# An attention and two MLPs on one core: 1/sqrt from a table, weight halves spread over the blocks, results kept in SBUF

## The chip, the core and the metric

The kernel runs on one NeuronCore of a Trainium2 chip. Its engines work from queues of their own, each in the order in which the program gives its instructions: PE (TensorE, matrix products), DVE (VectorE) and ACT (ScalarE) for elementwise work, POOL (GpSimd) and SP, which here issue transfers (DMAs). The metric is device time in microseconds (us) of one execution.

## The reference

```python
def _attn_ref(q, k, v, g_norm):          # q, k, v: (8, 8, 576, 64) fp32
    kv = np.einsum('bhsd,bhse->bhde', k, v)
    out = np.einsum('bhsd,bhde->bhse', q, kv)
    rms = np.sqrt(np.mean(out * out, axis=-1, keepdims=True) + 1e-06)
    return (out / rms * g_norm).astype(np.float32)
...
x = attn_out.transpose(0, 2, 1, 3).reshape(4608, 512)
gate = 1.0 / (1.0 + np.exp(-(x @ w_gate)))           # w_gate, w_val: 512 x 1536
x = (gate * (x @ w_val)) @ w_out                     # w_out: 1536 x 512
...
h = x @ w_in                                         # w_in: 512 x 2048
g = np.where(h >= 1, h, np.where(h <= -1, 0.0, (h + 1) ** 2 / 4))
return g @ w_out                                     # w_out: 2048 x 512
```

## The kernel before, in words

Every fp32 product is made as three products of fp32r halves: a value is split into a high half (`hi`, a copy on ACT) and the rest (`lo`, a subtraction on DVE), and `mm3` (L82 to L86) adds hi x hi, hi x lo and lo x hi. `split` (L70) is that pair of instructions.

The 4608 tokens are 9 blocks of 512. The first MLP takes a block in 12 chunks of 128 of its 1536 hidden columns. For a chunk, `gate_value` sums the gate into PSUM bank h0 and the value into bank h1 (12 matmuls each), ACT takes the sigmoid of h0 (L441), DVE multiplies it by h1 (L443, `gf`). `split_g` and `split_wo` make the halves gh, gl of that product and woh, wol of the output weights, and `down` adds the chunk's projection into four banks (12 matmuls). There is one h0 and one h1, so the next chunk's gate waits until the sigmoid has read the last.

The order in each queue is the order of the code. In blocks 2 to 7, chunk f issues in turn: the gate of chunk f + 1 with its sigmoid and splits; a piece of the next block's attention (`late_piece`; even chunks take one of four pairs of heads, odd chunks its norm: a sum of squares on PE, `inv_rms`, and later a Newton step); the projection of chunk f; and some steps of preparing the second MLP's weights (`w2_steps`). At a block's end, `store` evacuates the four banks and sends them to DRAM (`x2d`), and the next block's first gate follows.

The weights of the second MLP arrive as 64-bit floats. `decode_steps` turns a tile into fp32 on ACT and DVE in 6 steps. An "in" unit decodes two tiles, makes four sums and differences (for a Strassen-like product), and splits and stores four pairs of halves to `w2d`; an "out" unit decodes one, splits and stores it to `wo2d` (`halves_out`). There are 8 in and 16 out units. In `halves_out` each high half is written over a tile that the pair before has just stored, so a split waits until those stores have landed. Before, `run(work, 6)` follows each chunk and the rest of a block's three or four units is run at its end; the last three units lie in block 8.

Block 8's 12 products are stored to DRAM (`gd`) and loaded again for its projection, beside which the second MLP starts: `Second.begin` loads the first x (`x_load`) and the first weights (`w_load`, tile `wst`), and `x_steps` makes the x halves. The second MLP takes 6 groups of 768 tokens. A group has 8 chain sets of 7 products (`product`, L556) in banks A, B, C, D, each set with its own `wst` (1.8 MB, two buffers), and then 16 output products. A set's last product and the next set's first both use bank A.

Of the kernel before, what the change touches and what calls it, by code (L numbers as in the profile page):

```python
# [15 lines left out]
P = 128  # L16
# [16 lines left out]
def attn_gated_mlp_kernel(ctx: ExitStack, tc: tile.TileContext, a: dict, out: bass.AP):  # L33
# [45 lines left out]
    def temp(name, tag, **kw):  # L79
        return tp.tile([P, T], F32, name=name, tag=tag, **kw)  # L80
# [26 lines left out]
    def load_q(j, p, early=False):  # L107
        t = wp.tile([P, T], F32, name="q_early", tag="w") if early else temp("qraw", "qraw", bufs=2)
        nc.sync.dma_start(out=t, in_=a["qT"][p, :, j * T:(j + 1) * T])
        qraw[j, p] = t  # L110
# [52 lines left out]

    def inv_rms(SS, m, r):
        nc.vector.tensor_scalar(out=m, in0=SS, scalar1=1.0 / D, scalar2=EPS, op0=ALU.mult, op1=ALU.add)
        nc.scalar.activation(out=r, in_=m, func=AF.Sqrt)
        nc.vector.reciprocal(out=r, in_=r)

    def newton(m, r, t):

# [137 lines left out]
    def run(steps, n=None):  # L308

        while n != 0 and next(steps, steps) is not steps:  # L310
            n = n and n - 1
# [70 lines left out]
    def load_raw_w2():  # L382
        if w2_todo:
            key = w2_todo.pop(0)
            load_raw(key, a["w_2"][key[1:]])

    def halves_out(src, place, dst):

        hi, lo = place.bitcast(F32R), src.bitcast(F32R)
        yield split(src, hi, lo)  # L390
        for h, t in enumerate((place, src)):
            d = dst(h)
            nc.sync.dma_start(out=d, in_=t if len(d.shape) == 2 else t.rearrange("p (o n) -> p o n", n=2 * P))
        yield
        yield

    def w2_steps(unit):
# [30 lines left out]
    def gv_sum(f, i, xs, bank=None, between=None):  # L428
        if bank is None:
            t = h_p.tile([P, T], F32, name=f"h{i}", tag=f"h{i}")  # L430
        else:
            t = acc_p.tile([P, T], F32, name=f"h{i}", tag=f"acc{bank}")
        for c in range(KC):
            mm3(t, wgv[f, i], xs[c], c == 0, c == KC - 1, slice(c * P, (c + 1) * P))
            if between and c == KC // 2 - 1:
                run(between, 1)
        return t

    def gv_act(gate, value, tag="gf"):
        sig = temp("sig", "sig")  # L440
        nc.scalar.activation(out=sig, in_=gate, func=AF.Sigmoid)  # L441
        g = temp("gf", tag, bufs=1 if tag == "gf" else 2)
        nc.vector.tensor_tensor(out=g, in0=sig, in1=value, op=ALU.mult)  # L443
        return g

    def gate_value(f, xs, banks=(None, None), tag="gf"):
        return gv_act(*(gv_sum(f, i, xs, banks[i]) for i in range(2)), tag)

    def split_g(j, f, g):
        gs[j, f] = split(g, half_tile(gp, "gh", "gh"), half_tile(gp, "gl", "gl"))  # L450
# [16 lines left out]
    def store(dst, tags=("dt", "du", "dt", "du")):  # L467
        for c in range(4):
            t = temp("ev", tags[c], bufs=2 if tags[c] in ("dt", "du") else 1)
            (act_copy if c % 2 else dve_copy)(t, acc[c])  # L470
            nc.sync.dma_start(out=dst(c), in_=t)


    class Second:
# [23 lines left out]

        def bank(self, tag):
            return self.ch_p.tile([P, T], F32, name=f"ch{tag}", tag=tag)  # L500


        def w_load(self, s):
# [94 lines left out]
        def rest(self):  # L598
            self.wo2p = self.pool("wo2", 1, "left")
            self.gst = self.pool("gst", 1, "left")  # L600
            self.gsp = self.pool("gsp", 4, "left")
            self.acc_p = self.pool("acc2", 1, "left", space=bass.MemoryType.PSUM)
            self.wo2 = {}
            self.wo2_load(0)
            self.wo2_load(HF)
            groups = NT // (2 * T2)
            for g in range(groups):
                self.group(g, g + 1 < groups)
            self.stack.close()

        def group(self, g, more):
# [1 line left out]
            acc = [self.acc_p.tile([P, T], F32, name=f"acc2_{t}", tag=f"acc2_{t}") for t in range(3)]  # L613
            late = None
            for s in range(HF):
                A, D, B, C = (self.bank(n) for n in "ADBC")
                self.ws = self.w_next
                if s + 1 < HF:
                    self.w_next = self.w_load(s + 1)
                    if g == 0:  # L620
                        self.wo2_load(s + 1)
                        self.wo2_load(s + 1 + HF)
                elif more:
                    x = self.x_load(g + 1)
                c0 = self.tmp.tile([P, 2, T2], F32, name="c0", tag="c0", bufs=2)
# [51 lines left out]
            self.out_product(acc, HF - 1, this_hi, False, False)  # L677
            ready[1] = self.high(src(order[1]))
            self.low(ready[1], src(order[1]))
            acc2 = [self.bank("B"), self.bank("C"), self.acc_p.tile([P, T], F32, name="acc2_3", tag="acc2_3")]  # L680
            if more:
                steps = self.x_steps(x)
                self.w_next = self.w_load(0)
# [22 lines left out]
    with tc.manual_schedule():  # L706
# [197 lines left out]
            if f == F1 - 1:  # L904
                store(lambda c: x2d[j][:, c, :], ("du", "sig", "du", "gf"))
        split_wo(wo, 0)
        share = {j: n for j, n in zip(range(2, NB), (3, 4, 3, 4, 3, 4, 3))}

        def w2_work(j):
            for unit in w2_units[sum(share[i] for i in range(2, j)):][:share[j]]:  # L910
                yield from w2_steps(unit)

        last = NB - 1
        load_raw_w2()
        for j in range(2, last):
            work = w2_work(j)
            for f in range(F1):
                if j + 2 < B and f in (0, 2, 4, 6):
                    load_kv(j + 2, f // 2)
                if f + 1 < F1:  # L920
                    g = gate_value(f + 1, xs)
                    split_g(j, f + 1, g)
                    split_wo(wo, f + 1)
                if f < 9:
                    late_piece(j + 1, f)
                    if f % 2 and j + 2 < B:
                        kv_product(j + 2, f // 2)
                down(j, f)
                if f == F1 - 2:
                    split_x()  # L930
                run(work, 6)
                if f == F1 - 1:
                    run(work)
                    store(lambda c: x2d[j][:, c, :])
                    if j + 1 < last:
                        split_wo(wo, 0)
                        split_g(j + 1, 0, gate_value(0, xs))
                    if j + 2 < NB:
                        load_q(j + 2, 0)
                        load_q(j + 2, 1)  # L940

        work = w2_work(last)
        for f in range(F1):
            keep_g(0, f, gate_value(f, xs, tag="wol"))
            run(work, 6)
            if f >= F1 - 3:
                load_g(0, f - F1 + 3)
        run(work)
        early_end.close()
        second = Second()  # L950
        split_g(last, 0, gf[0, 0])
        split_wo(wo, 0)
        load_g(0, 3)
        second.begin()
        for f in range(F1):
            if f + 1 < F1:
                split_g(last, f + 1, gf[0, f + 1])
                split_wo(wo, f + 1)
            if 0 < f < F1 - 3:
                load_g(0, f + 3)  # L960
            if f > 1:
                run(second.xsteps, 1)
            down(last, f)
        store(lambda c: x2d[last][:, c, :])
        run(second.xsteps)
        first_part.close()
        second.rest()

# [39 lines left out]
```

## Time and profile before

| | |
|---|---|
| time, three runs | 1835.89 us median (1834.65 to 1841.38) |
| the profiled execution | 1834.16 us, span 1832.4 us |
| PE busy | 1771.7 us (97%) |
| DVE, ACT busy | 1092.5 us (60%), 790.8 us (43%) |
| mean granted clock of PE | 0.988 |
| DMA | 233.28 MB, all but 1.4 MB on SP's queue |

The span is the time from the first to the last instruction. "Idle before <- X" is the time that an engine stood before an instruction, and what released it. The granted clock is 1.00 at 2.4 GHz and 0.50 at 1.2 GHz. Blocks 0 and 1 run to about 300 us, blocks 2 to 7 from there to about 955, block 8 to 1062, the second MLP from there to the end.

### The profile page before, as it was taken

What the parts mean: (1) busy time and instruction counts of PE and PEld (TensorE: products, weight loads), DVE (VectorE), ACT (ScalarE), POOL (GpSimd) and SP (SyncE); (2) the same over time, 40 slices, a digit from 0 to 9 for tenths busy, and PEclk for the clock granted to TensorE, in tenths of its full rate; (3) what the DMA queues carried; (4) which work ended last, traced back from release to release, by engine and by line L of the source; (5) the groups of instructions that cost most, each with busy time, mean ns of one, the idle gap of its engine ahead of it and who ended that gap; (6) DMA issues with size and microseconds to landing.
All of it is one profiled execution on the core that took longest, in us unless ns stands there. A gap on an engine that the chain in (4) does not pass through costs nothing.

```text
span 1832.4 us, 22307 instructions
## 1 busy us (share of the span) xinstructions
PE 1771.7 (97%) x8560; PEld 1489.7 (81%) x8560; DVE 1092.5 (60%) x1817; ACT 790.8 (43%) x1361; POOL 2.0 (0%) x10
## 2 busy tenths in 40 slices
PE   8999999999989999999999899999999999999999
PEld 5787787787767887878778689889899898898897
DVE  3788756756657586665664545655555556456453
ACT  4454344534445455454542334434444344344342
POOL 0000000000000000000000000000000000000000
PEclk9999999999989999999999999999999999999999
DMA  7454633222242222211223466254344343342430
GB/s 220 151 194 161 208 101 112 86 89 85 74 130 89 77 90 92 77 63 58 86 71 136 161 248 250 82 188 153 113 165 163 103 159 130 138 161 93 178 121 35
DMA packets 85403, 233.28 MB, mean 127 GB/s; under 512 B 8488, under 2 KB 36264, under 8 KB 79152
## 3 DMA queue, kind: packets, MB, share of 16 engines
q1 hardware_dynamic: 85296, 231.85, 37.3%
q8 instruction: 67, 1.10, 0.2%
q14 instruction: 40, 0.33, 0.1%
HBM read 179.91 MB, written 51.90 MB: 127 GB/s over the span
## 4 chain that ended last, share of the span: by engine, by line
PE 50%; DVE 5%; DMA 3%; ACT 2%; issue 1%; SPq 0%; DVEq 0%; ACTq 0%
PE chA L556 8%; PE acc L86 6%; PE acc L85 6%; PE acc L84 6%; PE chB L556 5%; PE chD L556 3%; PE h L84 3%; PE chC L556 2%; PE h L86 2%; PE h L85 2%; DMA wst<-w2d 2%; PE chC L85 1%; PE chB L85 1%; PE chC L86 1%; PE chB L86 1%
## 5 line engine op out<-in xcount | busy, mean ns | idle before, releaser
L84 PE MATMUL h<-xh,w 128*128 128x512 f32 x768 | 307.3, 400 | 27.3 <-ACT sig L441 27.3
L86 PE MATMUL h<-xh,w 128*128 128x512 f32 x768 | 303.8, 396 | 0.2 <-DVE w L73 0.2
L85 PE MATMUL h<-xl,w 128*128 128x512 f32 x768 | 303.6, 395 | 0.0
L84 PEld LDWEIGHTS h<-xh,w 128*128 128x128 f32 x768 | 147.1, 192 | 66.6 <-ACT sig L441 35.1
L84 PE MATMUL acc<-gh,woh 128*128 128x512 f32 x432 | 178.0, 412 | 4.4 <-ACT woh L65 4.4
L86 PEld LDWEIGHTS h<-xh,w 128*128 128x128 f32 x768 | 147.0, 191 | 32.0 <-DVE w L73 0.6
L85 PE MATMUL acc<-gl,woh 128*128 128x512 f32 x432 | 171.7, 397 | 1.4 <-DVE gl L73 1.2
L86 PE MATMUL acc<-gh,wol 128*128 128x512 f32 x432 | 172.4, 399 | 0.5
L85 PEld LDWEIGHTS h<-xl,w 128*128 128x128 f32 x768 | 147.2, 192 | 30.6
L443 DVE TENSOR_TENSOR gf<-sig,h 128x512 f32<-128x512 f32 x108 | 74.0, 686 | 140.1 <-PE h L86 117.5
L86 PE MATMUL acc<-wo,gh 128*128 128x512 f32 x384 | 151.1, 393 | 0.0
L85 PE MATMUL acc<-wo,gh 128*128 128x512 f32 x384 | 150.9, 393 | 0.0
L84 PE MATMUL acc<-wo,gh 128*128 128x512 f32 x384 | 149.6, 389 | 0.0
L556 PE MATMUL chA<-x_t,wst 128*128 128x384 f32 x576 | 116.6, 337 | 0.0
L65 ACT ACTIVATE gh<-gf 128x512 fp32r<-128x512 f32 x72 | 45.6, 633 | 153.7 <-DVE gf L443 153.7
L441 ACT ACTIVATE sig<-h 128x512 f32<-128x512 f32 x108 | 64.1, 593 | 104.1 <-PE h L86 95.6
L556 PEld LDWEIGHTS chA<-x_t,wst 128*128 128x128 f32 x576 | 102.6, 188 | 3.7
L84 PEld LDWEIGHTS acc<-gh,woh 128*128 128x128 f32 x432 | 81.6, 189 | 25.0 <-ACT woh L65 5.3
L85 PEld LDWEIGHTS acc<-gl,woh 128*128 128x128 f32 x432 | 81.9, 190 | 22.1 <-DVE gl L73 2.8
L86 PEld LDWEIGHTS acc<-gh,wol 128*128 128x128 f32 x432 | 81.5, 189 | 22.0 <-DVE wol L73 2.8
L491 DVE TENSOR_TENSOR c<-chD,p 128x384 f32<-128x384 f32 x48 | 26.8, 558 | 110.6 <-ACT v L568 89.2
L65 ACT ACTIVATE u<-chA 128x384 f32<-128x384 f32 x96 | 47.1, 491 | 102.4 <-PE chA L556 102.4
(171 smaller groups left out, 3210.1 us busy)
## 6 DMA issues: line engine op xcount, KB each, us to landing
wst<-w2d SPq DMA_DIRECT2D x48, 1792.0 KB, 7.5
raw<-in_w SPq DMA_DIRECT2D x32, 512.0 KB, 4.6
raw<-in_w_gv SPq DMA_DIRECT2D x24, 512.0 KB, 4.4
kvraw<-in_kv_main SPq DMA_DIRECT2D x24, 448.0 KB, 4.6
gd<-gf SPq DMA_DIRECT2D x36, 256.0 KB, 3.4
gload<-gd SPq DMA_DIRECT2D x36, 256.0 KB, 3.0
x2d<-ev SPq DMA_DIRECT2D x36, 256.0 KB, 2.7
xin<-x2d SPq DMA_DIRECT2D x36, 256.0 KB, 4.9
```

The lines of the kernel that those rows point to most:

```text
L65: nc.scalar.activation(out=o, in_=i, func=AF.Copy)
L84: nc.tensor.matmul(ps, w[0][:, wsl], x[0], start=first, stop=False)
L85: nc.tensor.matmul(ps, w[0][:, wsl], x[1], start=False, stop=False)
L86: nc.tensor.matmul(ps, w[1][:, wsl], x[0], start=False, stop=last)
L441: nc.scalar.activation(out=sig, in_=gate, func=AF.Sigmoid)
L443: nc.vector.tensor_tensor(out=g, in0=sig, in1=value, op=ALU.mult)
L491: nc.vector.tensor_tensor(out=o, in0=x, in1=y, op=op)
L556: nc.tensor.matmul(bank[:, :T2], self.ws[w][h][:, sl], self.xo[x][:, l, c], start=first and c == n == 0, stop=c == 1 and n == 2, skip_grou ...
```

## The change

The diff has these parts.

- `inv_rms` takes 1/sqrt from ACT's table (`Abs_reciprocal_sqrt`) in place of a square root and DVE's reciprocal. The Newton step after it is as before.
- `halves_out` stores through POOL's queue, and has one empty step fewer.
- The steps of all weight units are one sequence that runs on over blocks 2 to 7, with a table of how many steps follow each chunk (`steps_beside`). A block's evacuations use four tiles of the norm and the product in place of the decode's, and the q loads of the block after next come after chunk 8.
- Block 8's products stay in SBUF (`kept`).
- The second weights of the second MLP are loaded during block 8's projection (`w_after`), and the first output weights after that.
- Chain sets use bank A and a second bank (`acc2_3`) in turn for the first product.

```diff
     def inv_rms(SS, m, r):
         nc.vector.tensor_scalar(out=m, in0=SS, scalar1=1.0 / D, scalar2=EPS, op0=ALU.mult, op1=ALU.add)
-        nc.scalar.activation(out=r, in_=m, func=AF.Sqrt)
-        nc.vector.reciprocal(out=r, in_=r)
+        nc.scalar.activation(out=r, in_=m, func=AF.Abs_reciprocal_sqrt)
...
         yield split(src, hi, lo)
         for h, t in enumerate((place, src)):
             d = dst(h)
-            nc.sync.dma_start(out=d, in_=t if len(d.shape) == 2 else t.rearrange("p (o n) -> p o n", n=2 * P))
-        yield
+            nc.gpsimd.dma_start(out=d, in_=t if len(d.shape) == 2 else t.rearrange("p (o n) -> p o n", n=2 * P))
         yield
...
+        def spare(self, n):
+
+            if n == 0:
+                return self.bank("A")
+            return self.acc_p.tile([P, T], F32, name="acc2_3", tag="acc2_3")
...
-            self.wo2_load(0)
-            self.wo2_load(HF)
...
-                A, D, B, C = (self.bank(n) for n in "ADBC")
+                A = self.spare((g + s) % 2)
+                D, B, C = (self.bank(n) for n in "DBC")
                 self.ws = self.w_next
                 if s + 1 < HF:
-                    self.w_next = self.w_load(s + 1)
+                    self.w_next = self.w_load(s + 1) if g + s else self.w_after
                     if g == 0:
-                        self.wo2_load(s + 1)
-                        self.wo2_load(s + 1 + HF)
+                        for f in range(0 if s == 0 else s + 1, s + 2):
+                            self.wo2_load(f)
+                            self.wo2_load(f + HF)
...
-            acc2 = [self.bank("B"), self.bank("C"), self.acc_p.tile([P, T], F32, name="acc2_3", tag="acc2_3")]
+            acc2 = [self.bank("B"), self.bank("C"), self.spare(g % 2)]
...
-        share = {j: n for j, n in zip(range(2, NB), (3, 4, 3, 4, 3, 4, 3))}
-
-        def w2_work(j):
-            for unit in w2_units[sum(share[i] for i in range(2, j)):][:share[j]]:
+        def w2_work():
+            for unit in w2_units:
                 yield from w2_steps(unit)
+
+        steps_beside = (5, 6, 3, 6, 3, 6, 3, 6, 3, 7, 3, 4)
...
-                run(work, 6)
+                if f == 8 and j + 2 < NB:
+                    load_q(j + 2, 0)
+                    load_q(j + 2, 1)
+                run(work, steps_beside[f])
                 if f == F1 - 1:
-                    run(work)
-                    store(lambda c: x2d[j][:, c, :])
+                    store(lambda c: x2d[j][:, c, :], ("sq", "sqh", "sql", "gf"))
...
-        work = w2_work(last)
+        run(work)
+        kept = {}
         for f in range(F1):
-            keep_g(0, f, gate_value(f, xs, tag="wol"))
-            run(work, 6)
-            if f >= F1 - 3:
-                load_g(0, f - F1 + 3)
-        run(work)
+            if f < 8:
+                if f % 2 == 0:
+                    two = tp.tile([P, 2, T], F32, name="kept", tag="raw", bufs=4)
+                kept[f] = two[:, f % 2]
+            else:
+                kept[f] = temp("kept", ("sq", "sqh", "sql", "qraw")[f - 8], bufs=2 if f == F1 - 1 else 1)
+            gate_value(f, xs, g=kept[f])
         early_end.close()
         second = Second()
-        split_g(last, 0, gf[0, 0])
+        split_g(last, 0, kept[0])
...
+            if f == 9:
+                second.w_after = second.w_load(1)
             down(last, f)
```

The change moves instructions in three places that the prediction speaks of. The first is DVE in chunk 5 of block 2, before (the chunk in which the timeline above 342 us lies) and then with the change. `m` and `r` belong to the norm, `dt` and `du` to a weight tile, `gf`, `gl` and `wol` to the chunk.

```order
L443 TENSOR_TENSOR gf<-sig,h_3024 128x512
L73 TENSOR_TENSOR gl<-gf,gh 128x512
L73 TENSOR_TENSOR wol<-wo,woh 128x512
L165 TENSOR_SCALAR m<-SS 128x512
L167 RECIPROCAL r<-r 128x512
L68 COPY kvbd_151<-kvps 64x64 x2
L294 TENSOR_SCALAR dt<-dt 128x512
L297 SCALAR_TENSOR_TENSOR dt<-raw,dt 128x512
L300 TENSOR_TENSOR du<-du,dt 128x512
```

```order
L442 TENSOR_TENSOR gf<-sig,h_3013 128x512
L73 TENSOR_TENSOR gl<-gf,gh 128x512
L73 TENSOR_TENSOR wol<-wo,woh 128x512
L165 TENSOR_SCALAR m<-SS 128x512
L68 COPY kvbd_151<-kvps 64x64 x2
L290 TENSOR_SCALAR du<-dt 128x512
L293 TENSOR_SCALAR dt<-dt 128x512
L296 SCALAR_TENSOR_TENSOR dt<-raw,dt 128x512
L299 TENSOR_TENSOR du<-du,dt 128x512
```

The reciprocal is gone, and other steps of a weight tile stand behind the copies of kv.

The second place is ACT at the end of block 3, before and then with the change: the last chunks' sigmoids, the four splits of an "in" unit (`dt<-dt 128x256` to `su<-su`), the halves of x for the next block (`xh`) and the evacuations (`ev`).

```order
L441 ACTIVATE sig<-h_4258 128x512
L65 ACTIVATE gh<-gf 128x512
L65 ACTIVATE woh<-wo 128x512
L65 ACTIVATE xh_4308<-xn 128x512
L65 ACTIVATE xh_4312<-xn 128x512
L65 ACTIVATE xh_4316<-xn 128x512
L65 ACTIVATE xh_4320<-xn 128x512
L65 ACTIVATE dt<-dt 128x256
L65 ACTIVATE dt<-dt 128x512
L65 ACTIVATE dt<-su 128x512
L65 ACTIVATE su<-su 128x512
L65 ACTIVATE ev<-acc_3542 128x512
```

```order
L65 ACTIVATE dt<-dt 128x256
L65 ACTIVATE dt<-dt 128x512
L65 ACTIVATE dt<-su 128x512
L65 ACTIVATE su<-su 128x512
L439 ACTIVATE sig<-h_4269 128x512
L65 ACTIVATE gh<-gf 128x512
L65 ACTIVATE woh<-wo 128x512
L65 ACTIVATE xh_4319<-xn 128x512
L65 ACTIVATE xh_4323<-xn 128x512
L65 ACTIVATE xh_4327<-xn 128x512
L65 ACTIVATE xh_4331<-xn 128x512
L287 ACTIVATE dt<-raw 128x512
```

The four splits stand ahead of chunk 11's sigmoid where they stood ahead of the evacuations.

The third place is SP around block 8's projection, before and then with the change: loads of x and weights (`xin`, `wst`), of block 8's products (`gload`), stores of `x2d` and loads of output weights (`wo`).

```order
L505 DMA wst<-w2d_86 128x3584
L454 DMA gload<-gd_4_114 128x512
L454 DMA gload<-gd_5_115 128x512
L454 DMA gload<-gd_6_116 128x512
L454 DMA gload<-gd_7_117 128x512
L454 DMA gload<-gd_8_118 128x512
L454 DMA gload<-gd_9_119 128x512
L454 DMA gload<-gd_10_120 128x512
L454 DMA gload<-gd_11_121 128x512
L471 DMA x2d_142<-ev 128x512 x4
L591 DMA wo_0_8571<-wo2d_94 128x1024
L591 DMA wo_8_8573<-wo2d_102 128x1024
```

```order
L510 DMA wst<-w2d_86 128x3584
L510 DMA wst<-w2d_87 128x3584
L470 DMA x2d_142<-ev 128x512 x4
L596 DMA wo_0_8515<-wo2d_94 128x1024
L596 DMA wo_8_8517<-wo2d_102 128x1024
L596 DMA wo_1_8519<-wo2d_95 128x1024
```

The loads of products are gone, and the second weights stand ahead of the stores of `x2d`.

## Rows read from the trace of the kernel before

**Rows 1.** The waits, all engines: who waited for whom, us in total, times, longest.

```profile
ACT dt L65 <- DMA w2d<-dt: 34.2, 10, 6.1
...
PE h L84 <- ACT sig L441: 27.3, 15, 10.2
...
PE chA L556 <- DMA wst<-w2d: 11.4, 4, 4.0
...
PE acc L84 <- ACT woh L65: 4.4, 2, 4.2
```

**Rows 2.** The timeline from 326 to 343 us: start, us, engine, line, instruction [idle before].

```profile
327.09 0.58 ACT L441 ACTIVATE sig<-h 128x512 f32<-128x512 f32 x1
...
330.37 0.63 ACT L65 ACTIVATE gh<-gf 128x512 fp32r<-128x512 f32 x1 [2.71 <-DVE gf L443]
...
331.65 0.69 DVE L73 TENSOR_TENSOR wol<-wo,woh 128x512 fp32r<-128x512 f32 x1
...
332.96 0.63 ACT L166 ACTIVATE r<-m 128x512 f32<-128x512 f32 x1
...
339.96 0.63 ACT L65 ACTIVATE hi<-dt 128x512 fp32r<-128x512 f32 x1 [6.37 <-DVE dt L305]
340.61 1.28 ACT L441 ACT_TABLE_LOAD   x1
...
342.56 0.51 PE L84 MATMUL h<-xh,w 128*128 128x512 f32 x1 [2.30 <-ACT sig L441]
```

**Rows 3.** The timeline at the end of block 3, 493 to 513 us.

```profile
493.63 0.39 PE L84 MATMUL acc<-gh,woh 128*128 128x512 f32 x1
...
496.88 0.42 ACT L65 ACTIVATE dt<-dt 128x256 fp32r<-128x256 f32 x1 [1.83 <-DVE su L414]
...
501.64 0.39 PE L86 MATMUL h<-xh,w 128*128 128x512 f32 x1
...
503.93 0.69 DVE L73 TENSOR_TENSOR su<-su,dt 128x512 fp32r<-128x512 f32 x1 [2.96 <-ACT dt L65]
...
506.94 0.63 ACT L65 ACTIVATE su<-su 128x512 fp32r<-128x512 f32 x1 [3.05 <-DMA w2d<-su]
...
512.27 0.80 PE L84 MATMUL h<-xh,w 128*128 128x512 f32 x1 [10.25 <-ACT sig L441]
```

**Rows 4.** Four windows of 7 us: length, PE busy, PEclk, DMA share, GB/s.

```profile
512.27:519.27 7.00, 7.00 (x19) 0.58 0.81 222
...
913.64:920.64 7.00, 7.00 (x24) 0.76 0.31 100
1036.03:1043.03 7.00, 6.93 (x22) 0.76 0.27 75
1073.66:1080.66 7.00, 7.00 (x28) 0.76 1.02 427
```

**Rows 5.** Groups by line and form: busy us, mean ns | idle before.

```profile
L167 DVE RECIPROCAL r<-r 128x512 f32<-128x512 f32 x24 | 80.5, 3353 | 16.8 <-ACT r L166 16.8
...
L291 DVE TENSOR_SCALAR du<-dt 128x512 uint32<-128x512 uint32 x68 | 28.0, 421 | 12.1 <-ACT dt L288 5.6 <-DMA w2d<-su 5.4
```

**Rows 6.** The tile w2d, its stores on SP: issue ns min/median/max, first and last start.

```profile
L393 SPq DMA_DIRECT2D w2d<-dt x40: 320/360/457, 306.8 to 979.9; - x40
```

**Rows 7.** The timeline at the start of the last block's projections down.

```profile
1020.24 0.49 PE L85 MATMUL acc<-gl,woh 128*128 128x512 f32 x1 [1.20 <-DVE gl L73]
```

**Rows 8.** The timeline at chain set 1 of groups 0 and 1.

```profile
1073.66 1.58 PE L556 MATMUL chA<-x_b,wst 128*128 128x384 f32 x6 [3.97 <-DMA wst<-w2d]
...
1193.80 6.51 SPq L505 DMA_DIRECT2D wst<-w2d  x2
...
1201.60 1.30 PE L556 MATMUL chA<-x_b,wst 128*128 128x384 f32 x6 [1.65 <-DVE c L491]
```

**Rows 9.** The DMA issues: count, KB each, median us to landing.

```profile
wst<-w2d SPq DMA_DIRECT2D x48, 1792.0 KB, 7.5
...
wo<-wo2d SPq DMA_DIRECT2D x16, 512.0 KB, 9.0
```

## What the change is predicted to do

> **What bounds the kernel now.** PE (TensorE) sets the time, so the first view is the waits, read for PE alone. It stands 27.3 us in 15 pieces for ACT's sigmoid, 11.4 us in 4 for loads of wst, 4.4 us for ACT's woh [rows 1]. The sigmoid's waits lie in blocks 2 to 7: it reads bank h0, which the gate sum of the next chunk overwrites.
>
> The second view is the timeline of one of these gaps. The sigmoid runs at 327.09. ACT then does gh and woh and the root r, and stands 6.37 us until DVE has decoded a weight tile, which stood behind a reciprocal; ACT works in order, so its table load and the next sigmoid come late, and PE stands 2.30 us at 342.56 [rows 2]. The third is the end of block 3. Four splits of one weight unit stand there in a row, from 496.88 to 507.57. Each waits for the stores of the one before (last half done at 504.62, next split at 506.94: 2.3 us). The evacuations and the sigmoid are queued behind them, and PE stands 10.25 us [rows 3].
>
> Gaps cost more than they last. In the 7 us after the gaps at 512.27 and 913.64 the granted clock is 0.58 and 0.76: PE, after standing, runs partly at the lower level, 1.2 GHz. That loses 7 x 0.42 = 2.9 us and 7 x 0.24 = 1.7 us [rows 4]. The five gaps of over 2 us in the blocks split into two of the first kind and three of the second: 10.9 us. So the blocks lose 27.3 + 10.9 = 38.2 us.
>
> **The change part by part.** The sum is made against the profiled execution, 1834.2 us (span 1832.4 and 1.8 around it), 1.7 below the median of the runs shown.
>
> *1/sqrt.* 24 reciprocals of 3.35 us go, 80.5 us of DVE [rows 5]; ACT keeps one activation and one table load for each, as before. DVE is not the bound, so this counts only in gaps like that of [rows 2]: there DVE's decode, ACT's hi and the sigmoid come 3.35 us earlier, which is more than the 2.30 us of the gap.
>
> *Steps spread.* An "in" unit now has 24 steps (two decodes of 6, four sums, four splits with a store step each), an "out" unit 8: 8 x (24 + 16) = 320. The new table runs 55 a block, so all are done in block 7, chunk 9. Nothing is flushed at a block's end, and the last block has none. The gap of 10.25 us loses its cause.
>
> What is late next: a step between two splits is gone, so two splits in one chunk have only the landing of the stores between them, and ACT waits that out with the chunk's sigmoid behind it. Laying the 320 steps on the table I count 15 such waits in 12 chunks. How much cover there is comes from the rows: counted from a sigmoid's start, ACT is free at +4.4 (wol starts at +4.56, just behind woh), DVE at +5.25 (wol done), r is done at +6.5 [rows 2]; 12 matmuls of a bank or of a projection take 2.75 us (35 steps from 493.63 to 501.64, 0.229 each) [rows 3].
> - Block 3, chunk 9 has all four splits. As in [rows 3] they last 10.7 us, from +4.4, and 0.4 more since the first waits for wol: +15.5. The last sigmoid of the block, its product, gh and woh add 2.5: +18.0. PE wants them after a bank, a projection, a gate and a projection, 5 x 2.75 = +13.75. Gap 4.2.
> - Block 7, chunk 5 has three: from r, +6.5, three splits and two waits 8.0, table load and sigmoid 1.9: +16.4. PE wants h0 at 13.75 + 0.9 for four matmuls of the attention: gap 1.7.
> - Block 5, chunk 11 has two. DVE's four splits of x (0.69 each from +5.25) and three sums of 0.42 end at +9.3; first split, wait and second split take 3.3, two evacuations and woh 1.75, the sigmoid 0.6: +14.95 against 13.75. Gap 1.2.
> - Blocks 2 (chunks 3, 4) and 5 (chunks 2, 3) carry one wait into the next chunk: 1.1 us of cover is left by the same steps. The five others keep about 2.3.
>
> *Stores on POOL's queue.* 96 stores leave SP. No row shows one on POOL. From below: they land as on SP, 2.3 us after the last half. From above: the longest such wait on SP, 6.1 us [rows 1]. I take the row nearest, 2.3, and 0.72 more, as if each of a pair's two issues took twice SP's 0.36 [rows 6]. The gaps become 4.2 + 3 x 0.72, 1.7 + 2 x 0.72, 1.2 + 0.72 and twice 2 x 0.72 - 1.1: 6.4, 3.1, 1.9, 0.3, 0.3, together 12.0. The first two are of a length that lowered the clock (mean of the five 2.2 us), the third may be: 5.5 more. The blocks lose 17.5 instead of 38.2: gain 20.7.
>
> The Trainium skill ("SBUF — State Buffer", "SBUF: two separate sides") states that GpSimd writes the descriptors of POOL's DMAs and is locked out of SBUF while a VectorE instruction in a two-port mode runs. DVE's shift of one input takes 421 ns [rows 5]; by that rule a store would wait for its end, at most 0.42 more for each pair, which is the second rival's price. No row of before can show it.
>
> *Buffers and q loads.* A block's last evacuation now lies in gf's buffer, which the next block's first product writes: stored about 1 us after the projection and wanted 5.5 after it, so any landing under 4.5 us is hidden. The q loads move three chunks ahead on SP, behind nothing that waits: 0.
>
> *Last block.* 12 stores and 12 loads of g go. The wait of 4.2 us for woh was for a load of g (its clock loss is 1.7, [rows 4]); the 1.2 us at the first gl stays, since DVE still makes the last product before it [rows 7]. Gain 5.9.
>
> *Second MLP.* The wait of 3.97 us at chain set 1 goes [rows 8], with its 1.7 us of clock [rows 4], as the second wst now loads during the projection: gain 5.7. Behind this load on SP stand only the last stores of x2d. The first wo tile is issued behind these, some 1.2 us into set 0 (an evacuation of 0.6 and issues, an estimate), and wanted after ten products of six matmuls of 384 columns: 60 x 0.229 x 0.75 = 10.3 us. Even at before's median, 9.0 [rows 9], it is just in time, and a wst load that was in its way is gone.
>
> *Two first banks.* From group 1 on set 1 also waits for its wst: issued at 1193.80, landing 7.5 later [rows 9] at 1201.3, against PE's start at 1201.60 [rows 8]. So the free bank gives 0.3 in groups 1 and 2 (bounds 0 and the whole 1.65), nothing in the three groups where wst ended the wait: 0.5.
>
> Sum: 20.7 + 5.9 + 5.7 + 0.5 = 32.8; 1834.2 - 32.8 = 1801.4. I predict 1801.
>
> **Rivals.**
> - *The waits stay hidden or short*: stores land on POOL's queue as on SP, which gives gaps of 7.1 and one clock loss of 2.2: 1834.2 - 28.9 - 12.1 = 1793; or PE has more cover than I count and the blocks lose nothing: 1783.9. For it: only six of the fifteen waits exceed cover, by little in two chunks. Against: the four splits of [rows 3] take 10.7 us wherever they stand.
> - *POOL's stores wait for DVE*: 0.42 more a pair, 1.14 in all. Gaps 7.6, 4.0, 2.3 and 1.2 twice: 16.3, clock 3 x 2.2: 22.9. 1834.2 - 15.3 - 12.1 = 1807. For it: DVE is busy 1092.5 of 1832.4 us, so a store often meets it. Against: an instruction of that kind stands only in the decode, rarely beside a split.
> - *Stores on POOL's queue land as late as SP's worst* (6.1 instead of 2.3, 3.8 more): gaps 15.6, 9.3, 5.0, twice 2 x 3.8 - 1.1 = 6.5, and 1.5 in five more chunks: 50.4, clock 5 x 2.4 = 12: 62. 1834.2 + 62 - 38.2 - 12.1 = 1846, slower. It turns to slower from about 3.0 more a wait. Against: on SP only what stood behind other DMAs took that long, and POOL's queue has nothing else.
> - *The gaps of the second stage stay*: second wst or wo tiles late, their memory being freed late. 1801.4 + 5.7 = 1807.
> - *The reciprocal was not what held the sigmoid*: then four gaps as in [rows 2] stay at 2.3 and 1.7 of clock, 16 us: 1817.
>
> **How the numbers follow.** Forecast 0.42, hidden or short waits 0.28, stores waiting for DVE 0.13, second stage 0.06, reciprocal 0.06, late landing 0.05. The range goes from the hidden waits to a landing 1.5 us later a pair, twice what I take (gaps 19.9, clock 9: 1813): 1783 to 1814. About 0.5%, 9 us, is what a measurement here tells from no change: only the late landing can be slower or same; a mixture of rivals can come near. Faster 0.93, same 0.03, slower 0.04.
>
> **What would show it.** In the waits after: PE for the sigmoid 10 to 14 us in place of 27.3, the largest in block 3 and another in block 7; no wait for woh of 4 us; wst's in three to five pieces of about 2.5 us, none at 1074. ACT's waits for w2d should be two to three us each, and a POOL store's landing 2.4 to 3.2 us. Landing over 4 us, waits of over 1 us for the sigmoid in chunks other than those named, or a stall at the start of the second MLP would make the prediction wrong.

## The result, and the profile after

The changed kernel takes 1810.45 us (median of four runs, 1804.71 to 1815.61) against 1835.27 for the kernel before, run beside it: ratio 0.9861, 95% interval 0.9819 to 0.9903, so 1.4% faster. That is 9 us more than the forecast of 1801 and within its range. The profiled execution is the longest of the four, 1815.61 us (span 1813.8).

So that runs can be compared by place, each execution is cut in three. The first piece ends where SP begins to store block 1's results. The second, blocks 2 to 7 and the gates of block 8, ends at the first `gl` product of the last projection, the row of [rows 7]. The third is the rest. In each piece "gaps" are PE's waits of over 0.15 us, and "clock" is the time lost below the full granted clock (the sum over windows of 7 us of 7 x (1 - clock)). Some of it lies within gaps and is counted in both: 4.4 us of the 15.3 before, 1.9 of the 12.0 after. In the first piece the time in front of the first entry of the clock's record is taken at half clock, for the reason given in the last section.

| piece | before: us, gaps, clock | after: us, gaps, clock | gain | predicted |
|---|---|---|---|---|
| to block 1's stores | 272.9, 8.0, 19.7 | 277.9, 8.5, 24.0 | -5.0 | 0 |
| blocks 2 to 8's gates | 747.4, 28.2, 15.3 | 739.0, 24.1, 12.0 | 8.4 | 20.7 |
| last projection and second MLP | 812.2, 19.9, 5.1 | 796.9, 10.1, 0.0 | 15.3 | 12.1 |

The blocks gave less than half of what was predicted, the end somewhat more. What PE waits for answers to [rows 1] (us in total, times, longest):

```profile
PE acc L84 <- ACT woh L65: 11.5, 4, 6.6
PE h L84 <- ACT sig L439: 5.6, 3, 3.2
PE chA L561 <- DMA wst<-w2d: 5.1, 3, 2.4
PE h L84 <- DVE gf L442: 5.1, 3, 2.8
...
PE SS L238 <- ACT sqh L65: 2.0, 1, 2.0
```

The sigmoid's 27.3 us are 5.6, but woh has taken 11.5 and gf, which PE never waited for before, 5.1. The gaps of block 3 and block 7 stand where they were expected (timeline; idle time and releaser in brackets), as [rows 3] did at 512.27:

```profile
498.70 0.80 PE L84 MATMUL acc<-gh,woh 128*128 128x512 f32 x1 [6.64 <-ACT woh L65]
...
909.42 0.63 ACT L65 ACTIVATE su<-su 128x512 fp32r<-128x512 f32 x1 [3.87 <-DMA w2d<-su]
911.36 0.60 ACT L439 ACTIVATE sig<-h 128x512 f32<-128x512 f32 x1
...
912.01 0.50 PE L84 MATMUL h<-xh,w 128*128 128x512 f32 x1 [3.15 <-ACT sig L439]
```

In the second half of these rows a split's high half waits 3.87 us for the stores of the split before it, and the sigmoid and PE's next gate stand behind it. Before, the same wait was 3.05 [rows 3].

The next rows are the end of block 5. The evacuations (`ev`), which I had taken to be stored 1 us after the projection, are copied by DVE only at 728.10, behind the chunk's splits; SP sends the four in order, and the next block's first product, which writes the buffer of the fourth, waits for its landing:

```profile
728.10 1.28 DVE L68 COPY ev<-acc 128x512 f32<-128x512 f32 x2
728.81 2.61 SPq L470 DMA_DIRECT2D x2d<-ev  x4
...
734.57 0.69 DVE L442 TENSOR_TENSOR gf<-sig,h 128x512 f32<-128x512 f32 x1 [4.58 <-DMA x2d<-ev]
...
735.31 0.80 PE L84 MATMUL h<-xh,w 128*128 128x512 f32 x1 [2.80 <-DVE gf L442]
```

The third kind of gap was in no step of mine. It is in block 3 and, larger, in block 6:

```profile
413.04 1.44 POOL L392 DMA_DIRECT2D w2d<-su  x2 [3.07 <-ACT su L65]
...
417.15 0.43 DVE L290 TENSOR_SCALAR du<-dt 128x512 uint32<-128x512 uint32 x1 [3.69 <-DMA w2d<-su]
...
423.33 0.50 PE L238 MATMUL SS<-sqh,ones 128*128 128x512 f32 x1 [1.97 <-ACT sqh L65]
```

```profile
819.89 0.63 ACT L65 ACTIVATE dt<-su 128x512 fp32r<-128x512 f32 x1 [3.84 <-DMA w2d<-dt]
...
821.54 0.72 POOL L392 DMA_DIRECT2D w2d<-su  x1
...
826.39 0.63 ACT L65 ACTIVATE su<-su 128x512 fp32r<-128x512 f32 x1 [3.36 <-DMA w2d<-su]
...
829.08 1.43 POOL L392 DMA_DIRECT2D w2d<-su  x2 [6.82 <-issue]
...
831.78 0.43 DVE L290 TENSOR_SCALAR du<-dt 128x512 uint32<-128x512 uint32 x1 [4.03 <-DMA w2d<-su]
...
833.31 0.68 DVE L442 TENSOR_TENSOR gf<-sig,h 128x512 f32<-128x512 f32 x1
...
835.23 0.80 PE L84 MATMUL acc<-gh,woh 128*128 128x512 f32 x1 [4.44 <-ACT woh L65]
```

In block 6 an "in" unit's last split ends at 827.02 on ACT. The next weight tile's decode follows in the same chunk and writes `du`, whose memory is still being stored, so DVE stands 4.03 us with gf queued behind it; in block 3 it is the same decode, with 3.69. Two more things make block 6's gap long. The store issued at 821.54 released ACT's next split only at 826.39, 4.85 us later. And POOL's store at 829.08 began 2.06 us after its half was ready; in the other 47 pairs the first store begins 0.29 to 0.31 after it.

The gaps cost clock as in [rows 4] (windows of 7 us after two of them: length, PE busy, PEld, DVE, ACT, POOL, PEclk, DMA share, GB/s):

```profile
498.70:505.70 7.00, 7.00 (x22) 5.53 (x23) 6.86 (x13) 4.31 (x8) 0.00 (x0) 0.69 0.10 35
...
835.23:842.23 7.00, 7.00 (x19) 5.45 (x20) 6.23 (x12) 4.51 (x9) 1.20 (x2) 0.59 0.06 25
```

POOL's store instructions (tile w2d: ns min/median/max) answer to [rows 6]: 0.7 us where SP took 0.36. Landing, issue to data, is 2.6 us for 256 KB at the median, but 22 of the 96 stores took 3.2 to 5.7 us, 14 of them over 4. Every one of the 22 had a packet of an instruction queue in flight, or a transfer that SP had issued within the 4 us before it or while it was under way. The 47 stores that had neither landed in 2.0 to 2.9 us.

```profile
L392 POOL DMA_DIRECT2D w2d<-dt x40: 540/707/729, 316.4 to 905.8; - x40
```

In the third piece the wait for gl stands as before [rows 7], that of 4.2 for woh and that of 3.97 at chain set 1 [rows 8] are gone, and chain set 1 of groups 1 to 5 waits as follows (the first of five):

```profile
1186.03 1.28 PE L561 MATMUL chA<-x_b,wst 128*128 128x384 f32 x6 [1.49 <-DMA wst<-w2d]
```

### The profile page after: what moved, and what is told of

It reads as the page before. It is cut to its first block, busy times and chain, and to the rows that moved or that the text cites. A ratio compares the mean times of both kernels' runs of the same rounds, so it can differ in the third digit from the quotient of the medians.

```text
span 1813.8 us, 22229 instructions
## 1 busy us (share of the span) xinstructions
PE 1766.6 (97%) x8560; PEld 1488.3 (82%) x8560; DVE 1010.0 (56%) x1792; ACT 790.3 (44%) x1361; POOL 63.0 (3%) x106
## 4 chain that ended last, share of the span: by engine, by line
PE 70%; issue 21%; DMA 3%; POOL 2%; DVE 2%; ACT 1%; SPq 0%; POOLq 0%; DVEq 0%; ACTq 0%
PE acc L86 7%; PE acc L84 7%; PE acc L85 7%; PE h L84 6%; PE h L86 6%; PE h L85 6%; PE chB L561 5%; PE chA L561 4%; PE acc L561 4%; PE chD L561 3%; PE chC L561 3%; DMA wst<-w2d 2%; POOL w2d L392 2%; PE X L144 1%; PE chC L86 1%
## 5 line engine op out<-in xcount | busy, mean ns | idle before, releaser
L84 PE MATMUL acc<-gh,woh 128*128 128x512 f32 x432 | 179.9, 417 | 11.5 <-ACT woh L65 11.5
L442 DVE TENSOR_TENSOR gf<-sig,h 128x512 f32<-128x512 f32 x96 | 65.8, 686 | 142.1 <-PE h L86 107.2
L86 PE MATMUL acc<-wo,gh 128*128 128x512 f32 x336 | 132.4, 394 | 0.0
L85 PE MATMUL acc<-wo,gh 128*128 128x512 f32 x336 | 132.2, 394 | 0.0
L84 PE MATMUL acc<-wo,gh 128*128 128x512 f32 x336 | 130.9, 390 | 0.0
L490 DVE TENSOR_TENSOR gh<-c,gh 128x384 fp32r<-128x384 f32 x96 | 53.6, 558 | 57.4 <-ACT gh L65 56.7
L73 DVE TENSOR_TENSOR gl<-gf,gh 128x512 fp32r<-128x512 f32 x72 | 49.8, 692 | 50.3 <-ACT gh L65 50.3
L73 DVE TENSOR_TENSOR wol<-wo,woh 128x512 fp32r<-128x512 f32 x108 | 73.9, 684 | 0.6 <-ACT woh L65 0.6
```

The source lines that it names most:

```text
L73: nc.vector.tensor_tensor(out=lo, in0=src, in1=hi.bitcast(F32), op=ALU.subtract)
L84: nc.tensor.matmul(ps, w[0][:, wsl], x[0], start=first, stop=False)
L85: nc.tensor.matmul(ps, w[0][:, wsl], x[1], start=False, stop=False)
L86: nc.tensor.matmul(ps, w[1][:, wsl], x[0], start=False, stop=last)
L490: nc.vector.tensor_tensor(out=o, in0=x, in1=y, op=op)
```

## Experiments

The first four kernels shared their runs of before (1835.9 us), the next four theirs (1833.6), the last four theirs (1838.3). "Stretch" is the second piece, "rest" the third. The ratio is to the kernel before, with its 95% interval.

| kernel | us | ratio | start | stretch, gaps, clock | rest |
|---|---|---|---|---|---|
| the change again | 1815.1 | 0.9877 (0.9846 to 0.9908) | 280.4 | 738.8, 23.8, 12.0 | 796.2 |
| its stores on SP | 1797.4 | 0.9786 (0.9754 to 0.9817) | 280.6 | 723.1, 13.9, 3.4 | 795.9 |
| 4th evacuation in a raw tile | 1801.5 | 0.9818 (0.9786 to 0.9851) | 271.3 | 732.1, 19.4, 10.3 | 796.1 |
| one split in a chunk | 1802.4 | 0.9801 (0.9767 to 0.9835) | 279.6 | 727.6, 16.6, 6.9 | 797.6 |
| before + the table's 1/sqrt | 1808.2 | 0.9847 (0.9809 to 0.9885) | 262.4 | 717.8, 12.2, 5.1 | 811.4 |
| one split, raw tile | 1780.0 | 0.9708 (0.9679 to 0.9737) | 277.0 | 706.8, 3.3, 0.0 | 795.2 |
| SP, raw tile | 1785.3 | 0.9737 (0.9705 to 0.9768) | 278.8 | 712.5, 7.3, 1.7 | 796.7 |
| one split, raw tile, SP | 1777.0 | 0.9696 (0.9663 to 0.9728) | 271.4 | 705.6, 2.6, 0.0 | 797.0 |
| the same, reciprocal back | 1787.5 | 0.9730 (0.9710 to 0.9749) | 268.1 | 711.0, 4.9, 0.0 | 797.3 |
| the change, bank A only | 1818.6 | 0.9891 (0.9872 to 0.9910) | 279.1 | 738.8, 23.7, 12.0 | 799.6 |
| the change, products via DRAM | 1821.0 | 0.9902 (0.9874 to 0.9930) | 275.5 | 741.1, 23.9, 15.3 | 805.9 |
| the change, second weights late | 1817.9 | 0.9877 (0.9838 to 0.9917) | 263.4 | 739.1, 23.8, 12.0 | 800.4 |

The stretch minus its gaps and clock lies between 700.5 and 706.1 in every kernel, so these two carry its differences. The start, whose instructions no experiment alters but for one norm, differs by 18 us from one execution to the next; that is why prices are read from the pieces and not from the medians alone.

**The change again.**

> The changed kernel once more. Theory (the half clock between 21 and 49 us is chance, the same code ran there at full clock before): 1808 us (1803 to 1813), the granted clock between 20 and 50 us near 1.00, the waits of PE in blocks 2 to 7 again 22 to 26 us; the POOL store that began 2 us late in block 6 is not late again, and its wait for woh falls from 4.4 to about 2.4. Rival (the change itself slows the start): again 0.5 to 0.6 there and 1815. Rival on the late store (a fixed effect of this order): again about 2 us late, 4.4 us.

The stretch agrees to 0.3 us. The start was slow again, but the full clock that the expectation gives to the kernel before was not there either (last section), and with the same code as here the start took 263.4 us in another run (second weights late). So nothing shows that the change slows it. The late POOL store was no chance: the 40th pair began 2.06 or 2.07 us after its half in all eight profiles with POOL's queue, also in the two with another table of steps (below), where it lies at a block's end. The rows are from the one with one split and the raw tile:

```profile
815.32 0.63 ACT L65 ACTIVATE su<-su 128x512 fp32r<-128x512 f32 x1 [4.15 <-DMA w2d<-su]
...
818.02 1.43 POOL L392 DMA_DIRECT2D w2d<-su  x2 [4.63 <-ACT sig L439]
```

With the change's table of steps a packet of an instruction queue begins 1.3 to 1.6 us before this store; with the other table none begins in the 12 us before it, and the delay is the same. So it goes with the place in POOL's order of instructions, and what makes it stays open.

**Stores on SP's queue.**

```diff
-            nc.gpsimd.dma_start(out=d, in_=t if len(d.shape) == 2 else ...
+            nc.sync.dma_start(out=d, in_=t if len(d.shape) == 2 else ...
```

> The changed kernel with the weight stores back on SP's queue. Theory (a store's issue costs 0.72 us on POOL and 0.36 on SP, and each wait between two splits holds two): each such wait shorter by 0.7 us, block 3's gap at chunk 11 from 6.6 to 4.5, block 7's from 3.2 to 1.8, waits for x2d unchanged at 5; with the clock 6 to 8 us less than the changed kernel, about 1802. Rival (on SP the stores stand behind loads and stores that wait, and loads stand behind them): waits between splits of up to 6 us as before, and 1812 or more.

The stretch is 15.7 us shorter, twice what was expected. The waits between splits are 3.0 and 3.1 where they were 3.8 and 3.9: the 0.7 was right. Block 3's gap is 4.50 (from 6.64), block 7's 1.48 (from 3.15). Two gaps are gone with their clock, each behind a decode that follows a unit's last split: that of 1.97 in block 3 and that of 4.44 in block 6. Block 6 in this kernel:

```profile
815.08 3.98 SPq L392 DMA_DIRECT2D w2d<-su  x3
...
817.32 0.63 ACT L65 ACTIVATE su<-su 128x512 fp32r<-128x512 f32 x1 [0.48 <-DMA w2d<-su]
...
820.28 0.43 DVE L290 TENSOR_SCALAR du<-dt 128x512 uint32<-128x512 uint32 x1 [1.61 <-DMA w2d<-su]
```

DVE's wait for `du` is 1.61 in place of 4.03 and PE does not wait there. The store issued at 815.08 released ACT at 817.32, after 2.24 us where POOL's took 4.85. So on POOL's queue a wait is 0.7 to 0.8 longer where a store lands as usual and over 2 us longer where it lands late or begins late, and waits add up along a chunk until they pass its cover. Late landings are rarer on SP's queue: over 3 us for 5 of the 80 stores whose landing the trace has. Here SP's loads are also issued in another order, behind the stores; a kernel with POOL's stores and that order of loads was not run.

**The fourth evacuation in another tile.** It goes to a `raw` tile, one of the four that raw weights are loaded into, in place of gf's buffer.

```diff
-                    store(lambda c: x2d[j][:, c, :], ("sq", "sqh", "sql", "gf"))
+                    store(lambda c: x2d[j][:, c, :], ("sq", "sqh", "sql", "raw"))
```

> The changed kernel with a block's fourth evacuation in half of a raw tile in place of gf's buffer. Theory (gf waits for the landing of that store): PE's 5.1 us for gf at the block ends go, and some 2 us of clock with them: 1803. Rival (DVE is late there because of its own steps, and gf comes no earlier): waits of 3 to 5 us at the block ends stay under another name, 1810.

As the theory had it: no wait for gf is left, and the stretch is 6.7 to 6.9 us shorter. The buffer, which I had costed at nothing, was worth that.

**One split in a chunk.**

```diff
-        steps_beside = (5, 6, 3, 6, 3, 6, 3, 6, 3, 7, 3, 4)
+        steps_beside = (6, 6, 6, 2, 2, 2, 8, 6, 2)
...
-                run(work, steps_beside[f])
+                run(work, steps_beside[((j - 2) * F1 + f) % 9])
```

> The changed kernel with the table 6, 6, 6, 2, 2, 2, 8, 6, 2, repeated every 9 chunks over all 72: at most one split in a chunk, and none followed in its chunk by a decode that reuses its memory. Theory (the gaps of blocks 2 to 7 are the waits between a store and the next use of its tile within a chunk): PE's waits for woh, the sigmoid and sqh, 19 us, fall under 4 us; those for gf at the block ends may stay, 3 to 5; with the clock 18 to 24 us less, about 1789. Rival (DVE is late in chunks with six to eight steps whatever waits there): waits move to these chunks and the gain is under 8 us, 1803 or more.

Half a hit. The waits for woh and sqh are gone and the sigmoid's are 3.3, as expected; but those for gf at the block ends grew to 13.3 us, more than the 3 to 5 allowed for. The first row is of the waits, and the others of the timeline at the end of block 3, of this kernel.

```profile
PE h L84 <- DVE gf L442: 13.3, 5, 3.4
```

```profile
500.75 1.28 DVE L68 COPY ev<-acc 128x512 f32<-128x512 f32 x2
501.47 2.56 SPq L470 DMA_DIRECT2D x2d<-ev  x4
...
507.83 0.69 DVE L442 TENSOR_TENSOR gf<-sig,h 128x512 f32<-128x512 f32 x1 [5.19 <-DMA x2d<-ev]
```

The last chunk has no gate beside it, so a split there and one in the chunk before are still close: the evacuations are late by them, and gf with them.

**The table's 1/sqrt alone, in the kernel before.**

```diff
-        nc.scalar.activation(out=r, in_=m, func=AF.Sqrt)
-        nc.vector.reciprocal(out=r, in_=r)
+        nc.scalar.activation(out=r, in_=m, func=AF.Abs_reciprocal_sqrt)
```

> The kernel before with the table's 1/sqrt alone. The stretch from block 1's stores to the last projection down took 747.4 us before. Theory (the reciprocal held the sigmoid in four gaps as at 342 us, 2.3 us and 1.7 of clock each): 16 us less, 731 there, PE's waits for the sigmoid from 27.3 to about 12, the 10.2 at the end of block 3 left; 1820 in all. Rival (what holds DVE and ACT there is the order of the splits, and the reciprocal is hidden): 744 or more, 1832.

A miss of both, on the far side: the stretch is 29.6 us shorter (gaps 16.0, clock 10.2, 3.4 not placed), and this one line is worth as much as the whole change. The sigmoid's waits are 11.7 us, of which 10.3 are the block end:

```profile
PE h L84 <- ACT sig L440: 11.7, 3, 10.3
```

Why it gave so much is seen in a weight's split at the start of block 2, first before, then here:

```profile
311.10 0.62 ACT L65 ACTIVATE dt<-dt 128x512 fp32r<-128x512 f32 x1
311.23 3.35 DVE L167 RECIPROCAL r<-r 128x512 f32<-128x512 f32 x1 [0.70 <-ACT r L166]
...
314.93 0.69 DVE L73 TENSOR_TENSOR dt<-dt 128x512 fp32r<-128x512 f32 x1
...
317.85 0.63 ACT L65 ACTIVATE dt<-su 128x512 fp32r<-128x512 f32 x1 [6.13 <-DMA w2d<-dt]
```

```profile
299.66 0.62 ACT L65 ACTIVATE dt<-dt 128x512 fp32r<-128x512 f32 x1
...
300.31 0.69 DVE L73 TENSOR_TENSOR dt<-dt 128x512 fp32r<-128x512 f32 x1 [0.86 <-ACT dt L65]
...
303.29 0.63 ACT L65 ACTIVATE dt<-su 128x512 fp32r<-128x512 f32 x1 [3.01 <-DMA w2d<-dt]
```

The reciprocal stood between the two halves of a split. The low half, its store and the next split came 3 us later, and the wait that is booked under the transfer, 6.13, is 3.01 without it.

**One split and the raw tile, on POOL's and on SP's queue.** The edits are those above, together.

> The changed kernel with one split in a chunk (the 9-chunk table) and the fourth evacuation in a raw tile, stores on POOL's queue. The stretch from block 1's stores to the last projection: 739 with the change, 727.6 with the 9-chunk table. Theory (of that kernel's losses 13.3 us are gf's waits for the fourth store, with 3 to 5 of clock): 710 to 713, and 1786 in all, faster than both kernels. Rival (the gate after a block's end then waits for the evacuations or the split beside them): 720 or more, 1796.

> One split in a chunk, the raw tile, and the stores on SP's queue. Theory (POOL's queue costs only where a tile is used again in the same chunk, and there is no such place here): within 3 us of the same kernel on POOL's queue, 709 to 713 for the stretch. Rival (POOL's queue costs something everywhere): 5 to 15 us less than on POOL's queue.

Both run as the theory said, a little better: 706.8 and 705.6, no clock lost, and only the sigmoid still waited for in the stretch (waits of the second):

```profile
PE h L84 <- ACT sig L439: 2.6, 2, 1.3
```

POOL's queue costs 1.2 us here, against 15.7 with the change's table of steps and 19.6 (732.1 to 712.5) with the raw tile: it costs much only where a tile is written again in the same chunk. Both kernels beat the changed one and the one before; the faster takes 1777.0 us, 3.0% less than before.

**SP's queue and the raw tile, with the change's own table.**

> The changed kernel with its own table, the weight stores on SP's queue and the fourth evacuation in a raw tile. Same stretch: 723.1 with SP alone, 732.1 with the raw tile alone, 739 with neither. Theory (two separate losses, which add): 715 to 717, 1790 in all. Rival (on SP's queue the raw tile's load stands behind the evacuation's landing and holds up the stores): 722 or more.

712.5, 3.9 us less than the two prices would give from 738.9 (15.7 and 6.8). So the two losses add, with 3.9 us more that are not placed. The spread of the steps was not run alone. The nearest is this kernel, which has the change's other parts too, against the table's 1/sqrt alone: 712.5 against 717.8, so 5.3 us, and 12.2 with one split in a chunk on SP's queue (705.6).

**The reciprocal back, in the fastest kernel.** Its edit is the inverse of the table's.

> The kernel with one split in a chunk, the raw tile and SP's stores, with the square root and DVE's reciprocal back in place of the table. The stretch from block 1's stores to the last projection took 705.6 us with the table. Theory (a reciprocal costs where it stands between a split's two halves or in front of a decode that the next sigmoid waits for, whatever the table of steps): 715 to 725, with waits for the sigmoid of 1 to 3 us each. Rival (with one split in a chunk the 3.35 us are hidden everywhere): 709 or less.

Between the two: 5.5 us more in the stretch. With one split in a chunk most of a reciprocal is hidden; in the order of the kernel before it cost 29.6.

**The parts of the end, each undone in the changed kernel.** Bank A for every set:

```diff
-                A = self.spare((g + s) % 2)
-                D, B, C = (self.bank(n) for n in "DBC")
+                A, D, B, C = (self.bank(n) for n in "ADBC")
```

> The changed kernel with every chain set's first product in bank A again. The stretch from the last projection down to the end took 796.9 and 796.2 us with the change, 812.2 before. Theory (the second bank gives 0.5): 797 to 798. Rival (the free bank saves the wait at the start of every group, 1.65 us each): 803 or more.

Block 8's products through `gd`:

```diff
-            gate_value(f, xs, g=kept[f])
+            keep_g(0, f, gate_value(f, xs, tag="wol"))
```

> The changed kernel with block 8's products stored to DRAM and loaded again. Theory (the wait of 4.2 us for a loaded product and 1.7 us of clock come back): 802.4 for the stretch from the last projection to the end, with a wait for woh of about 4 us some 16 us after its start. Rival (without the weight stores and the last weight units beside block 8 the loads come in time): 797.

The second weights in the first set:

```diff
-            if f == 9:
-                second.w_after = second.w_load(1)
...
-                    self.w_next = self.w_load(s + 1) if g + s else self.w_after
+                    self.w_next = self.w_load(s + 1)
```

> The changed kernel with the second weights of the second MLP loaded at the start of its first set. Theory (PE stands 4 us at chain set 1 as before, with 1.7 of clock): 802.2 for the stretch from the last projection to the end. Rival (the earlier load only moved the wait to the first output weights, so nothing is lost): 797.

Against 796.5 (the mean of the change's two runs): bank A +3.0, DRAM +9.4, late weights +3.9, together 16.3 where before and after differ by 15.6. One row of each shows the wait that came back: at chain set 1 of group 0 for the bank and for the late weights, some 16 us into the last projections for the products:

```profile
1062.17 0.44 PE L561 MATMUL chA<-x_b,wst 128*128 128x384 f32 x1 [1.17 <-DVE g L490]
```

```profile
1033.15 0.80 PE L84 MATMUL acc<-gh,woh 128*128 128x512 f32 x1 [4.98 <-ACT woh L65]
```

```profile
1048.07 0.44 PE L561 MATMUL acc<-x_b,wst 128*128 128x384 f32 x1 [2.50 <-DMA wst<-w2d]
```

Of the first two numbers part is clock (1.7 and 5.1 us up to the last product, 0.0 in the change), and 1.7 of each lies at about 1570 us, after a wait of 2.0 to 2.1 us in group 4 that the change's two runs have too, where it lowered no clock. So the bank's price is 1.3 to 3.0, and that of the products 7.6 to 9.4. In groups 1 to 5 set 1 waits 8.3 us with bank A and 7.9 and 8.7 in the change's two runs: there the second bank gives nothing that can be told from chance.

## Why the prediction was right, and where it was not

- *1/sqrt.* Right in its mechanism and mis-sized. I took it to remove four gaps of 2.3 us and their clock, 16 us (the last rival's price); alone, in the order of the kernel before, it gives 29.6. The row that I used as the upper bound of a store's landing, 6.1 us [rows 1], was not a slow transfer but the reciprocal's. The chain of waits of the kernel before has the reciprocal with 4.5 to 7.8% of each 100 us from 700 to 1000 us, and the prediction leaves that out.
- *Steps spread.* Right for the chunks whose splits I laid out: 6.64 and 3.15 against 6.4 and 3.1, and 1.34 against 1.9 for the sigmoid at the end of block 5. Wrong for "the five others keep about 2.3": one of these chunks lost 1.97 (block 3), the chunk behind another lost 4.44 (block 6), and the carried wait in block 5 cost 1.06, not 0.3. In both I had counted splits only; a decode after a unit's last split waits for the same stores, and DVE's wait for w2d stood in [rows 5] with 5.4 us.
- *Stores on POOL's queue.* 0.72 more in each wait was right where a store lands as usual (3.87 against 3.05). What it costs was not: my terms make 8.2 us of it (gaps 12.0 - 7.1, clock 5.5 - 2.2), the run on SP 15.7, since the chunks that I held to be covered were not. "They land as on SP" failed there: the stores at 413.04 (block 3) and 821.54 (block 6) landed after 3.99 and 4.77 us, where the same two took 2.17 and 2.21 on SP's queue, and the one at 829.08 began 2 us late. The Trainium skill ("DMA: Bandwidth & Descriptors", "Issuing engine by pattern") calls the SP path generally faster than GpSimd's; the trace agrees, with landings of 2.2 and 2.6 us for 256 KB, but in a kernel without such waits it makes 1.2 us.
- *Buffers: hidden.* Failed: 5.1 us of waits for gf, 6.7 with their clock. The step assumed an evacuation stored 1 us after the projection; DVE copies behind the chunk's splits, and the fourth store stands behind three others, issued 7.6 us after the projection's end in block 5.
- *Last block, second MLP.* Right: both waits are gone, and undone they come back, 9.4 and 3.9 against 5.9 and 5.7. *Two first banks.* 0.5 was low at most by 2.5, and for other waits than I named: the bank saves 1.17 at chain set 1 of group 0, which before lay under the 3.97 for wst. The end gave 15.3 for 12.1; 1.7 of the 3.2 more is clock, of which it lost none.
- *Clock in the blocks.* 5.5 predicted, 12.0 measured (10.1 outside the gaps), from twice the gaps: 24.1 for 12.0. The 10.9 taken for the kernel before was right: 15.3 less the 4.4 within gaps.
- *Rivals.* Stores waiting for DVE, by the rule of the Trainium skill ("SBUF — State Buffer", "SBUF: two separate sides"), would have begun, or landed, up to 0.42 us later in some pairs than in others. All but one begin 0.29 to 0.31 after their half, and without such packets or transfers none landed later than 2.9, so the trace does not bear it out. *Late landing* came in part: the longest in the change is 5.7 us, and the argument that POOL's queue has nothing else did not hold, since transfers of other queues in flight went with every late one. In the kernel with one split and the raw tile landings reach 6.3 us and cost nothing. The second stage's gaps did not stay.
- *Signs.* PE's waits for the sigmoid came to 5.6 us where 10 to 14 were expected, two waits for woh of over 4 us came where there was to be none, and 14 stores took over 4 us to land, which was named as a sign of error. So the time came out within the range, and the mechanism in part.

The blocks' error of 12.3 us was partly given back by the end's 3.2, and the start, which the forecast did not consider, added 5.0 in this execution. That the total came so near was in part luck: the reciprocal's 29.6 us paid for what the new table of steps, gf's buffer and POOL's queue cost, from 717.8 with the table's 1/sqrt alone to 739.0 in the change.

## What to carry to other kernels

When a wait is booked under a transfer, look at when the stored data was ready before taking it as a landing time: a 3.35 us instruction on an engine that is 60% busy doubled it, and taking that instruction out was worth as much as the whole change. Where a tile is written over after its store, put the store and the next write in different pieces of work; then neither the queue's issue time nor its landing matters. Count every reuse of the memory, the decode's and the evacuation's too, not only that of the instruction that the change moves.

## What the runs showed of the hardware

- The start ran at half clock for a different time in each execution, with the same instructions, and the profile does not show all of it. The window 40 to 50 us, first with the change and then with its stores on SP, where the code is the same up to block 2 (PEclk is the third number from the end):

```profile
40.00:50.00 10.00, 10.00 (x50) 7.42 (x49) 2.93 (x5) 3.91 (x9) 0.00 (x0) 0.55 0.00 0
```

```profile
40.00:50.00 10.00, 10.00 (x65) 8.09 (x62) 3.70 (x6) 6.22 (x14) 0.00 (x0) 1.00 0.01 2
```

  The 1.00 is no measurement. The record of the clock has its first entry at 51.9 us in the second trace (18.3 in the first, 40.2 before), and what lies in front of it counts as full, in the mean clock of an execution too. The products there follow each other by 0.43 us, as in the first trace at a recorded half clock (45.90 to 47.17), and by 0.23 us only later, as the second trace shows:

```profile
49.28 0.63 PE L84 MATMUL h<-xh,w 128*128 128x512 f32 x1
49.70 0.63 PE L85 MATMUL h<-xl,w 128*128 128x512 f32 x1
50.13 0.63 PE L86 MATMUL h<-xh,w 128*128 128x512 f32 x1
...
53.55 0.39 PE L86 MATMUL h<-xh,w 128*128 128x512 f32 x1
53.78 0.40 PE L84 MATMUL h<-xh,w 128*128 128x512 f32 x1
```

  With the time from PE's first instruction to the first entry taken at half clock, the first piece lost 6.2 to 27.2 us in the 14 profiles and took 262 to 281 us; without its gaps and this loss it is 245 to 248 us in every one. So the clock makes the start's scatter. What decides for how long it is low stays open.
- A store takes POOL 0.54 us to issue for 128 KB and 0.71 to 0.73 for 256 KB of w2d, whose rows go to two places, but 0.54 to 0.64 for 256 KB of wo2d, whose rows go to one. So it is not the size alone.

```profile
L392 POOL DMA_DIRECT2D wo2d<-hi x16: 540/547/555, 348.0 to 941.4; - x16
```

- Once in 48 pairs, at the same place in POOL's order in eight of eight profiles, a store began 2 us late.
- In all eight profiles with POOL's queue its stores landed in 2.0 to 3.2 us where no packet of an instruction queue and no transfer from SP was near, and in up to 6.3 us beside these. That these delay them is argued from this alone.
